# Attention and expert layer on one core: z products before block products, and 27 columns of counts moved behind the last numerators

## The chip, the cores and the metric

The kernel runs on one core of a Trainium2 chip. The metric is device time in microseconds of one execution, lower is better. Engines are named as the profile names them: PE (TensorE matmul), PEld (its weight load), DVE (VectorE), ACT (ScalarE), POOL (GpSimd), SP (SyncE, which here issues DMAs).

## The reference, cut to what matters

q, k and v have 8 batches, 8 heads, 576 positions and 64 channels; everything is float32.

```python
def phi(x):                                   # 64 -> 256 features
    proj = x @ w_phi                          # w_phi: 64 x 128
    proj = proj - max(abs(proj))              # over the 128 features
    return concat([exp(proj), exp(-proj)])
kv  = sum_s phi(k)[s,f] * v[s,d]              # block, 256 x 64, per head
z   = sum_s phi(k)[s,f]                       # 256, per head
out = (phi(q) @ kv) / (phi(q) @ z + 1e-6)     # numerator / denominator
x   = out as 4608 tokens x 512
# then an expert layer: logits = x @ w_gate (8 experts); tokens are given to experts in order of
# falling logit, 576 to each; out[token] = relu(x @ w1[e]) @ w2[e]
```

## The kernel before, in words

**Attention.** Two batches and two heads make one unit, 16 units in all (u = 0 to 15). A unit's steps carry short names, which the order table of the kernel uses too:

- `kt0`, `kt1`, `qt0`, `qt1`: DVE transposes of the loaded k and q (L178). `kg0`, `kg1`, `kg2` and `qg0`, `qg1`, `qg2`: PE projections, three groups of the nine positions tiles each (L189).
- `kgm`, `qgm`: DVE maximum (L194). `kgs2`, `qgs`: DVE subtraction (L197). For `kg0` and `kg1`, ACT copies out of PSUM (`kgc`, L203) and POOL subtracts (`kgs`, L206). `ke`: ACT exponentials (L218). `ad1` to `ad8`: POOL adds the nine tiles of phi(k) up (L226, L227), which is what z is made from.
- `kv0` to `kv2`: PE block sums over positions (L236). `kvt`: ACT copies them to SBUF as kvT (L240). `bd`: the block products, 32 PE instructions that spread the block and bring in the gate weights (L252). `kz`: ACT copies them into the tile kz (L255). `z`: the z products, 16 PE instructions of two columns (L265). `zk`: DVE puts z into the last column of kz (L267).
- `T0` to `T2`: PE transposes of q's projections (L281); `ex`: ACT exponentials (L285). `num0`, `num1`: the numerators with the denominator as their 73rd column (L298), which read kz. `x0`, `x1`: DVE division (L303 to L315); in the last unit ACT scales the rows instead (L314), reading the numerators from PSUM. `lg`: POOL adds the logits up. `st`: SP stores x.

Matmuls come in four shapes of the array: the page writes `64*64` (projections, kv, bd), `128*64` (z, numerators), `64*128` (T) and `128*8` (counts).

**Order.** All steps go into a planner (`Plan`, L18 to L99) with a due time from the table ATT; each engine executes its steps in the order of their due times, and a step whose inputs are late holds up everything behind it on its engine. In the steady stretch PE works on the projections of unit u+1 while it finishes unit u. PSUM is cut into four pairs of banks, g0 to g3; every PE step takes one pair, the one that by the plan comes free first (L93), and the pair is free again when its reader is done.

**The bridge to the experts.** The expert layer first sorts tokens by counting: digits of the logits are compared with thresholds, and PE counts the comparisons per expert. For the first 27 of the 36 columns of tokens (units 0 to 11) the comparisons are made by DVE while attention still runs (steps `pr0` to `pr5`, function prep0, L483 on). Their counts are the PE steps `cnt0`, `cnt1`, `cnt2` of nine matmuls each (L517), placed in attention's table, and the DVE step `n0` (L519) saves their sum. After the last numerators eleven matmuls of ones keep PE busy (`warm`, L321), while DVE makes x, logits and the comparisons of the last nine columns; then come nine counts (L517), whose result is compared with capacity less the saved sum (L639). Five further digits follow, each with 36 counts (L622), filler matmuls (`fill`, L588) and short DVE steps, until the first expert is known and its weights can be loaded. The eight experts' products (L935, L966, L981) fill the rest. The routing's PSUM tiles come from a pool that takes over attention's eight banks: the count tile (`rps`) lies in the banks that were g0, the filler's tile (`y1`) in a bank that was g1. A block of small DVE steps that prepares constants (`init`, L415 to L560) stands, by its due time, behind the last zk and ahead of the last x0.

Of the kernel before, what the change touches and what calls it, by code (L numbers as in the profile page):

```python
# [100 lines left out]
def attention(ctx, tc, nc, q, k, v, w_phi, w_gate, xs, L, C, xp, cfg={}, after=None, later=None, count=None, init=iter(())):  # L101
# [42 lines left out]
    def pair(u_):  # L144
        return lambda x: ps.tile([128,2,512],F32,name='g%d'%x['buf'][u_],bufs=1)
# [11 lines left out]
    def unit(u):  # L157
# [84 lines left out]
        add('kvt','ACT',ac(512),kend,kvt,[('kv',2)],frees=(('g',u,'kv'),))  # L242
        def bd(x):
            p=T['bdp',u]=pair(('g',u,'bd'))(x)
            t=T['kvT',u]
            for i in range(2):
                for fh in range(2):
                    for a in range(2):
                        r=slice(64*a,64*a+64)
                        for c in range(2):  # L250
                            o=128*fh+64*c
                            PE.matmul(p[64*c:64*c+64,a,72*(2*i+fh):72*(2*i+fh)+72],t[r,i,o:o+64],C['bd'][r,272*hp+72*i:272*hp+72*i+72],start=True,stop=True)  # L252
        def kz(x):
            t=T['kz',u]=sb.tile([128,2,2,2,73],F32,name='kz',bufs=2)
            A.copy(t.rearrange('p i h a e -> p a (i h) e')[:,:,:,0:72],T['bdp',u][:,:,0:288].rearrange('p a (g e) -> p a g e',e=72))  # L255
        add('bd','PE',520.,kend+d['bd'],bd,['kvt'],'Q',slots(('g',NG,'bd')),ins=65)
        add('kz','ACT',ac(576),kend+d['bd']+.6,kz,['bd'],slot=slots(('kz',2)),frees=(('g',u,'bd'),))
# [8 lines left out]
        def zk(x):  # L266
            V.tensor_copy(T['kz',u].rearrange('p i h a e -> p (h a) i e')[:,:,:,72],T['zp',u][:,0,0:8].rearrange('p (g i) -> p g i',i=2))  # L267
        add('z','PE',450.,kend+d['z'],z,[('ad',8)],'B',slots(('g',NG,'z')),(('ks',u),),ins=33)
        add('zk','DVE',180.,kend+d['z']+.5,zk,['z','kz'],frees=(('g',u,'z'),))
# [19 lines left out]
        for g,(j0,j1) in enumerate(JG):  # L289
            n=j1-j0; due=d['num']+d['ns']*g  # L290
            js=sorted(set(j//3 for j in range(j0,j1)))
            def pe(x,g=g,j0=j0,j1=j1):
                p=T['np',u,g]=pair(('g',u,'num',g))(x)
                for a in range(2):
                    for j in range(j0,j1):
                        for fh in range(2):
                            for ab in range(2):
                                PE.matmul(p[64*ab:64*ab+64,a,73*(j-j0):73*(j-j0)+73],T['qP',u,j//3][:,fh,a,ab,j%3,:],T['kz',u][:,a,fh,ab,:],start=fh==0,stop=fh==1)  # L298
            def dve(x,g=g,j0=j0,j1=j1,n=n):
                p=T['np',u,g][:,:,0:73*n].rearrange('p a (j e) -> p a j e',e=73)  # L300
                rd=sb.tile([128,2,n,1],F32,name='rd',bufs=2)
                if u==0 and g==0: sb.tile([128,8],F32,name='xpad',bufs=1)
                V.tensor_scalar(rd,p[:,:,:,72:73],1e-6,None,op0=OP.add)  # L303
                V.reciprocal(rd,rd)
                if g==0: T['x',u]=(xp if lastu else sb).tile([128,9,144],F32,name='xp',bufs=1 if lastu else 2)
                x_=T['x',u]
                Lb=L[:,9*bp+j0:9*bp+j1,:]
                if lastu:
                    L3=C['L3'][:,j0:j1]
                    for a in range(2): V.tensor_mul(L3[:,:,:,1+a],p[:,a,:,64*a:64*a+8],rd[:,a].to_broadcast([128,n,8]))  # L310
                    V.tensor_reduce(Lb.rearrange('p j (e o) -> p j e o',o=1),L3,axis=AX.X,op=OP.add)
                    if g==1: after()
# [22 lines left out]
        if u==NU-NP-1:  # L335

            it=later(); z0=t0+d['num']+d['ns']+d['pr']; prev=('lg',u)
            for i,(e,dur) in enumerate((('DVE',600.),('DVE',1500.),('POOL',100.),('DVE',350.),('DVE',1400.),('POOL',100.))):
                def f(x,it=it): next(it,None)
                P.add((('pr',i),u),e,dur,place(('pr',i),e,u,z0+d['prs']*i),f,[prev],lat=95. if e=='DVE' else 30.,lock=i in(1,4)); prev=(('pr',i),u)  # L340
            for c in range(NB-1):
                def cp(x,c=c):
                    if c==0: T['cnt']=ps.tile([128,2,512],F32,name='g%d'%x['buf'][('g',u,'cnt')],bufs=1)[0:8,0,0:32]
                    count[1](T['cnt'],c,count[4](c),c==0,c==NB-2)
                P.add((('cnt',c),u),'PE',600.,place(('cnt',c),'PE',u,z0+d['prs']*(6+c)),cp,[(('pr',4),u)]+([(('cnt',c-1),u)] if c else []),lat=200.,mode='Z',slot=(('g',NG,('g',u,'cnt')),) if c==0 else (),ins=18)
            P.add(('n0',u),'DVE',150.,place('n0','DVE',u,z0+d['prs']*(6+NB)),lambda x: count[2](T['cnt']),[(('cnt',NB-2),u)],lat=95.,frees=(('g',u,'cnt'),))
    for u in range(NU): unit(u)
    P.by[(('x',0),NU-1)]['deps'].append(('n0',NU-NP-1))
# [44 lines left out]
def moe_consts(rp, nc, C, L, MC, cfg={}):  # L393
# [31 lines left out]
    spacer=rp.tile([1,1],F32,name='spacer'); rp.tile([128,64],F32,name='mpad')  # L425
# [136 lines left out]
def moe(ctx, tc, nc, L, xs, w1, w2, out, C, MC, R0, rt, cfg={}):  # L562
# [11 lines left out]
    state,prep,(cmp0,cnt0,put0,prep0),DIG,KW,kt,kl,scl,k0,e8,ones,tri,dif,onef,msk,Q,dup,dup2,ids,half,un,opn,spacer,tin,eye8,e8s,pid=MC  # L574
# [14 lines left out]
    def routing(r):  # L589
# [3 lines left out]
        if not last:  # L593
# [415 lines left out]
def tile_kernel(ctx, tc, q, k, v, w_phi, moe_w_gate, moe_w1, moe_w2, out):  # L1009
# [59 lines left out]
```

## Time and profile before

| what | value |
|---|---|
| three timed runs | 752.07, 752.39, 754.91 us; median 752.39 us |
| the profiled execution | 754.1 us, of which the span of its instructions is 752.1 us |
| PE busy | 737.7 us (98%) |
| DVE busy | 564.4 us (75%) |
| ACT busy | 348.6 us (46%) |
| POOL busy | 307.0 us (41%) |
| mean granted PE clock | 0.994 of full speed |

Attention takes the first 268 us of the span, the routing's first expert about 30 us, the experts the rest. A busy share is an average over these stages; the last PE instruction of one step and the first of the next tell more, since PE executes in order: where start follows start without a gap, the difference of two starts is what a step costs.

### The profile page before, as it was taken

How to read it: one execution, taken by the hardware profiler on the slowest of the kernel's cores; microseconds unless marked ns; L12 is line 12 of the kernel's file. 1: busy time of each engine (PE TensorE's matmuls, PEld its weight loads, DVE VectorE, ACT ScalarE, POOL GpSimd, SP SyncE). 2: the span in 40 equal slices, each digit the busy share in tenths (PEclk: the TensorE clock that was granted, in tenths of full speed). 3: DMA queues.
4: the chain of work that ended last, by engine and by line, in shares of the span. 5: the costliest groups of instructions: out<-in, count | busy, mean ns of one | idle time of the engine just before them, and what ended most of it. 6: DMA issues, size and time to landing. Idle time of an engine off the chain costs nothing.

```text
span 752.1 us, 25412 instructions
## 1 busy us (share of the span) xinstructions
PE 737.7 (98%) x10898; PEld 634.0 (84%) x10899; DVE 564.4 (75%) x1487; ACT 348.6 (46%) x616; POOL 307.0 (41%) x329
## 2 busy tenths in 40 slices
PE   7999999999999999999999999999999999999997
PEld 4788898889888876888997997897897897897985
DVE  7989989998898868876895894895895895663410
ACT  3777777777776522513513513512522522532411
POOL 5998988988889503004104104104104104302002
PEclk9999999999999899999999999999999999999999
DMA  9988988888873114406305305406306407661301
GB/s 161 162 153 174 166 168 155 161 157 148 155 166 76 34 34 147 142 13 205 135 27 192 133 17 202 134 4 213 135 2 208 143 1 225 235 183 52 133 15 50
DMA packets 241168, 94.29 MB, mean 125 GB/s; under 512 B 190512, under 2 KB 227664, under 8 KB 241056
## 3 DMA queue, kind: packets, MB, share of 16 engines
q1 hardware_dynamic: 230288, 73.09, 40.9%
q0 software_dynamic: 6096, 18.98, 7.5%
q8 instruction: 86, 1.41, 0.8%
q10 hardware_dynamic: 4672, 0.59, 0.6%
q14 instruction: 26, 0.21, 0.1%
HBM read 72.58 MB, written 20.05 MB: 123 GB/s over the span
## 4 chain that ended last, share of the span: by engine, by line
PE 79%; issue 11%; DVE 4%; DMA 2%; ACT 2%; POOL 2%; POOLq 0%; SPq 0%; ACTq 0%; DVEq 0%
PE h L935 21%; PE y L966 18%; PE g L298 10%; PE g L236 8%; PE g L189 7%; PE g L281 3%; PE y L981 3%; PE g L252 2%; PE rps L627 2%; DMA raww<-in_moe_w_dram 1%; PE g L265 1%; PE h L900 1%; ACT kvT L240 1%; PE rps L622 1%; POOL out_dram L996 1%
## 5 line engine op out<-in xcount | busy, mean ns | idle before, releaser
L996 POOL DMA_INDIRECT out_dram<-ysb,idx x40 | 39.2, 979 | 330.7 <-ACT ysb L989 327.4
L227 POOL TENSOR_TENSOR ks<-ks,kP 128x512 f32<-128x512 f32 x112 | 143.4, 1281 | 7.1 <-ACT kP L218 0.8
L935 PE MATMUL h<-xh,w1l 128*128 128x272 f32 (+3 forms) x512 | 140.9, 295 | 1.2 <-DVE w1l L853 1.2
L935 PE MATMUL h<-xh,w1h 128*128 128x272 f32 (+3 forms) x512 | 141.0, 301 | 0.0
L948 ACT ACTIVATE fh<-h 128x240 fp32r<-128x240 f32 (+2 forms) x128 | 49.0, 385 | 131.1 <-PE h L935 118.1
L966 PE MATMUL y<-w2h,fh 128*128 128x512 f32 x256 | 100.8, 398 | 0.0
L966 PE MATMUL y<-w2h,fl 128*128 128x512 f32 x256 | 99.5, 393 | 0.0
L966 PE MATMUL y<-w2l,fh 128*128 128x512 f32 x256 | 99.5, 394 | 0.0
L935 PEld LDWEIGHTS h<-xh,w1l 128*128 128x128 f32 x512 | 96.3, 188 | 2.2 <-DVE w1l L853 1.4
L935 PEld LDWEIGHTS h<-xh,w1h 128*128 128x128 f32 x512 | 95.3, 188 | 2.2 <-issue 0.9
L935 PE MATMUL h<-xl,w1h 128*128 128x272 f32 (+3 forms) x512 | 93.2, 297 | 0.0
L218 ACT ACTIVATE kP<-kgt 128x768 f32<-128x768 f32 x96 | 74.1, 838 | 19.4 <-POOL kgt L206 19.4
L952 DVE SCALAR_TENSOR_TENSOR fl<-h,fh 128x240 fp32r<-128x240 f32 (+2 forms) x128 | 53.1, 417 | 37.4 <-ACT fh L948 19.5
L298 PE MATMUL g<-kz,qP 128*64 128x73 f32 x2304 | 79.8, 230 | 0.0
L298 PEld LDWEIGHTS g<-kz,qP 128*64 128x64 f32 x2304 | 77.1, 139 | 1.9 <-issue 0.9
L285 ACT ACTIVATE qP<-g 128x768 f32<-128x768 f32 x96 | 71.1, 815 | 13.6 <-PE g L281 13.4
L935 PEld LDWEIGHTS h<-xl,w1h 128*128 128x128 f32 x512 | 76.1, 188 | 0.5
L989 ACT COPY ysb<-y 128x512 f32<-128x512 f32 (+1 forms) x40 | 21.8, 546 | 110.8 <-issue 58.8
L236 PE MATMUL g<-kP,vi 64*64 64x256 f32 x1152 | 70.3, 377 | 0.0
L966 PEld LDWEIGHTS y<-w2h,fl 128*128 128x128 f32 x256 | 48.2, 188 | 9.2 <-issue 0.4
L966 PEld LDWEIGHTS y<-w2l,fh 128*128 128x128 f32 x256 | 48.2, 188 | 9.0
L966 PEld LDWEIGHTS y<-w2h,fh 128*128 128x128 f32 x256 | 48.2, 188 | 8.4
(224 smaller groups left out, 1313.8 us busy)
## 6 DMA issues: line engine op xcount, KB each, us to landing
raww<-in_moe_w_dram SPq DMA_DIRECT2D x64, 512.0 KB
vi<-in_v_dram SPq DMA_DIRECT2D x64, 144.0 KB
xs<-xp SPq DMA_DIRECT2D x32, 288.0 KB
ki<-in_k_dram SPq DMA_DIRECT2D x62, 144.0 KB
qi<-in_q_dram SPq DMA_DIRECT2D x62, 144.0 KB
xl<-xd SPq DMA_DIRECT2D x4, 288.0 KB
xd<-xg SPq DMA_DIRECT2D x4, 256.0 KB
xg<-xs,idx POOLq DMA_INDIRECT x40
```

What stands on the lines that cost most here:

```text
L189: PE.matmul(p[64*bi:64*bi+64,a,128*(s-s0):128*(s-s0)+128],t[r,bi,s,:],C['w'][r,:],start=True,stop=True)
L218: for i in range(2): A.activation(o[:,:,:,128*i:128*i+128],t,AF.Exp,scale=1.0-2*i)
L227: else: G.tensor_add(ks,ks,kP[:,s])
L236: PE.matmul(p[64*a:64*a+64,i,0:256],v_[r,a,s,:],kP[r,s,a,:],start=s==0,stop=s==8,skip_group_check=True)
L281: PE.transpose(p[:,i,o:o+64],t[r,a,s],ident[r,r])
L285: for fh in range(2): A.activation(t[:,fh].rearrange('p i a s t -> p i (a s t)'),p,AF.Exp,scale=1.0-2*fh)
L298: PE.matmul(p[64*ab:64*ab+64,a,73*(j-j0):73*(j-j0)+73],T['qP',u,j//3][:,fh,a,ab,j%3,:],T['kz',u][:,a,fh,ab,:],start=fh==0,stop=fh==1)
L935: PE.matmul(p,ws[:,k,o:o+128],xx[:,k,o1:o2],start=n==0,stop=n==11)
L948: A.activation(hh[:,f,o1:o1+m1],p[:,0:m1],AF.Relu)
L952: V.scalar_tensor_tensor(hl[:,f,o1:o1+m1],p[:,0:m1],0.0,hh[:,f,o1:o1+m1],op0=OP.max,op1=OP.subtract)
L966: PE.matmul(p,hx[:,f,o:o+128],ws[:,f%2,:],start=n==0,stop=n==23)
L996: st=G.indirect_dma_start(out=ov,out_offset=bass.IndirectOffsetOnAxis(ap=iv,axis=0),in_=yv,in_offset=None)
```

## The change

**In the units 3 to 13** (`zf`): z no longer stands behind bd, but ahead of it. bd waits for z, kz for zk, and zk no longer for kz; numerators wait for both. **At the end:** the steps cnt0, cnt1, cnt2, n0 and warm leave attention's table; behind the last numerators, the routing now issues the 27 counts, five filler matmuls of 512 columns (`idle(5)`) and then the last nine counts into one PSUM tile, and compares it with capacity directly. **The table ATT** has new due times throughout. MOE, the table of the experts, is the same.

```diff
-def attention(..., after=None, later=None, count=None, init=iter(())):
+def attention(..., after=None, later=None, init=iter(())):
...
+        zf=2<u<NU-2
+        def kzt():
+            if ('kz',u) not in T: T['kz',u]=sb.tile([128,2,2,2,73],F32,name='kz',bufs=2)
+            return T['kz',u]
...
-        add('bd','PE',520.,kend+d['bd'],bd,['kvt'],'Q',slots(('g',NG,'bd')),ins=65)
-        add('kz','ACT',ac(576),kend+d['bd']+.6,kz,['bd'],slot=slots(('kz',2)),frees=(('g',u,'bd'),))
+        add('bd','PE',520.,kend+d['bd'],bd,['kvt']+(['z'] if zf else []),'Q',slots(('g',NG,'bd')),ins=65)
+        add('kz','ACT',ac(576),kend+d['bd']+.6,kz,['bd']+(['zk'] if zf else []),slot=() if zf else slots(('kz',2)),frees=(('g',u,'bd'),))
...
-        add('zk','DVE',180.,kend+d['z']+.5,zk,['z','kz'],frees=(('g',u,'z'),))
+        add('zk','DVE',180.,kend+d['z']+.5,zk,['z'] if zf else ['z','kz'],slot=slots(('kz',2)) if zf else (),frees=(('g',u,'z'),))
...
-            add(('num',g),'PE',n*515.,due,pe,['zk']+[('ex',j) for j in js],'B',...)
+            add(('num',g),'PE',n*515.,due,pe,['zk','kz']+[('ex',j) for j in js],'B',...)
...
-        if lastu:
-            def wm(x):
-                p=pair(('g',u,'warm'))(x)
-                for _ in range(11): PE.matmul(p[:,0],w[:,0:128],w,start=True,stop=True)
-            P.add(('warm',u),'PE',2400.,1e6,wm,[(('num',1),u)],...)
...
-            for c in range(NB-1):
-                def cp(x,c=c): ...
-                P.add((('cnt',c),u),'PE',600.,place(('cnt',c),'PE',u,...),cp,...)
-            P.add(('n0',u),'DVE',150.,place('n0','DVE',u,...),lambda x: count[2](T['cnt']),...)
...
-    P.by[(('x',0),NU-1)]['deps'].append(('n0',NU-NP-1))
+    P.by[(('x',0),NU-1)]['deps'].append((('pr',5),NU-NP-1))
...
                 if part:
                     p=rps([8,K])
-                    cnt0(R,p,NT//9-1,cmp0(R,NT//9-1),True,True)
+                    for b in range(NT//9-1): cnt0(R,p,b,R['cm'][b],b==0,False)
+                    idle(5)
+                    cnt0(R,p,NT//9-1,cmp0(R,NT//9-1),False,True)
...
-                        if part: V.scalar_tensor_tensor(fl,p,-float(cap),R['n0'],op0=OP.add,op1=OP.is_ge,accum_out=da)
-                        else: V.tensor_scalar(fl,p,float(cap),0.0,op0=OP.is_ge,op1=OP.add,accum_out=da)
+                        V.tensor_scalar(fl,p,float(cap),0.0,op0=OP.is_ge,op1=OP.add,accum_out=da)
...
-ATT = {...}
+ATT = {...}
```

What the new due times of ATT mean, sorted for each engine (a name with ' is of the next unit):

```
one steady unit, PE
  before  kg0' qg0' kg2' kv0 kg1' kv1 qg2' kv2 qg1' bd z T2' T0' num0 num1 T1'
  after   kg0' kg2' kv0 kg1' qg2' kv1 qg0' kv2 qg1' z bd T2' T0' num0 num1 T1'
one steady unit, DVE (after)
          kgm0' kgm2' kgs2' kgm1' qgm2' qgs2' qgm0' qgs0' zk qgm1' kt0'' qgs1' kt1'' qt0'' x0 qt1'' x1
POOL      before  ad6 kgs0' ad7 ad8 kgs1' ad1'..ad5' lg
          after   ad6 lg(u-1) ad7 kgs0' ad8 kgs1' ad1'..ad5'
SP        before  ldk ldq ldv st;  after  ldk st ldq ldv; the k of unit 14 is loaded right behind
          that of unit 7 and transposed in units 6 and 10
the end, PE (unit number behind the @)
  before  num0@14 num1@14 T1@15 cnt0 bd@15 cnt1 cnt2 z@15 T2@15 num0@15 num1@15 warm
  after   bd@14 bd@15 T0@14 z@14 T1@15 qg2@15 T2@14 num0@14 num1@14 T0@15 T2@15 z@15 num0@15 num1@15
the end, DVE (after)
          zk@14 qgm2@15 pr3 pr4 qgs2@15 x0@14 x1@14 zk@15 init x0@15 x1@15
```

## Rows read from the trace of the kernel before

**Rows 1.** Busy time by stretch: start:end, length, engines' busy us, clock, DMA.
```profile
20.00:40.00 20.00, 18.37 (x536) 15.97 (x532) 19.83 (x30) 15.04 (x21) 18.49 (x15) 1.00 0.91 163
97.74:113.20 15.46, 15.41 (x448) 13.73 (x445) 13.96 (x21) 11.65 (x16) 13.41 (x11) 1.00 0.86 168
```

**Rows 2.** Timeline of one steady unit: start us, busy us, engine, line, instructions.
```profile
67.51 0.83 PE L189 MATMUL g<-w,qT 64*64 64x128 f32 x24
...
68.17 0.83 PE L189 MATMUL g<-w,kT 64*64 64x128 f32 x24
...
71.13 2.64 POOL L227 TENSOR_TENSOR ks<-ks,kP 128x512 f32<-128x512 f32 x2
...
74.02 0.83 PE L189 MATMUL g<-w,qT 64*64 64x128 f32 x24
...
74.90 0.58 PEld L252 LDWEIGHTS g<-bd,kvT 64*64 64x64 f32 x32 [0.29 <-ACT kvT L240]
...
75.56 0.63 PE L265 MATMUL g<-sel,ks 128*64 128x2 f32 x16
75.70 0.65 ACT L255 COPY kz<-g 128x576 f32<-128x576 f32 x1 [0.85 <-PE g L252]
...
76.13 0.96 PE L281 MATMUL g<-ident,qgt 64*128 64x64 f32 x24
...
77.02 4.80 PE L298 MATMUL g<-kz,qP 128*64 128x73 f32 x144
...
81.75 0.58 PE L281 MATMUL g<-ident,qgt 64*128 64x64 f32 x12
```

**Rows 3.** Waits of the weight loads, 82 to 236 us: total, times, longest.
```profile
PEld g L252 <- ACT kvT L240: 2.9, 10, 0.3
```

**Rows 4.** PE timeline of unit 0: block products followed by the same shape.
```profile
21.02 0.73 PE L252 MATMUL g<-bd,kvT 64*64 64x72 f32 x32 [0.70 <-ACT kvT L240]
21.57 1.49 PE L189 MATMUL g<-w,kT 64*64 64x128 f32 x48
```

**Rows 5.** PE timeline from the end of unit 14's numerators to the last counts.
```profile
255.75 0.59 PE L281 MATMUL g<-ident,qgt 64*128 64x64 f32 x12
256.26 0.70 PE L517 MATMUL g<-cmp,OH 128*8 128x32 bf16 x9
257.18 0.73 PE L252 MATMUL g<-bd,kvT 64*64 64x72 f32 x32 [0.21 <-DVE rd L303]
257.84 1.26 PE L517 MATMUL g<-cmp,OH 128*8 128x32 bf16 x18
259.03 1.02 PE L265 MATMUL g<-sel,ks 128*64 128x2 f32 x16
259.98 0.90 PE L281 MATMUL g<-ident,qgt 64*128 64x64 f32 x12
260.81 7.21 PE L298 MATMUL g<-kz,qP 128*64 128x73 f32 x144
267.95 2.55 PE L321 MATMUL g<-warm 128*128 128x512 bf16 x10
270.73 0.71 PE L517 MATMUL rps<-cmp,OH 128*8 128x32 bf16 x9 [0.23 <-DVE cmp L514]
```

**Rows 6.** Busy time by stretch, as in rows 1, of the last unit.
```profile
259.00:266.00 7.00, 7.00 (x116) 6.84 (x116) 3.89 (x30) 1.51 (x2) 0.00 (x0) 0.51 0.38 87
```

**Rows 7.** Timeline of DVE and ACT in the last unit.
```profile
260.17 0.22 DVE L415 TENSOR_SCALAR kl<-ktf 128x128 bf16<-128x128 f32 x1
...
263.73 0.20 DVE L560 CAST ids<-idp 128x72 bf16<-128x72 int32 x1
...
266.87 3.79 ACT L314 ACTIVATE xp<-g,rd 128x64 f32<-128x64 f32 x18 [4.37 <-DVE L L310]
...
268.06 0.17 DVE L303 TENSOR_SCALAR rd<-g 128x8 f32<-128x8 f32 x1 [0.91 <-PE g L298]
...
269.12 0.23 DVE L438 TENSOR_REDUCE m<-L 128x9 f32<-128x72 f32 x1
```

More of the change, by code (lines that the diff above doesn't have):

```diff
@@ L99, in order, with attention @@
         return sorted(out,key=lambda x:(x['start'],x['n']))
-def attention(ctx, tc, nc, q, k, v, w_phi, w_gate, xs, L, C, xp, cfg={}, after=None, later=None, count=None, init=iter(())):
+def attention(ctx, tc, nc, q, k, v, w_phi, w_gate, xs, L, C, xp, cfg={}, after=None, later=None, init=iter(())):
     B,H,S,D=q.shape
@@ L253, in kz @@
         def kz(x):
-            t=T['kz',u]=sb.tile([128,2,2,2,73],F32,name='kz',bufs=2)
+            t=kzt()
             A.copy(t.rearrange('p i h a e -> p a (i h) e')[:,:,:,0:72],T['bdp',u][:,:,0:288].rearrange('p a (g e) -> p a g e',e=72))
-        add('bd','PE',520.,kend+d['bd'],bd,['kvt'],'Q',slots(('g',NG,'bd')),ins=65)
-        add('kz','ACT',ac(576),kend+d['bd']+.6,kz,['bd'],slot=slots(('kz',2)),frees=(('g',u,'bd'),))
+        add('bd','PE',520.,kend+d['bd'],bd,['kvt']+(['z'] if zf else []),'Q',slots(('g',NG,'bd')),ins=65)
+        add('kz','ACT',ac(576),kend+d['bd']+.6,kz,['bd']+(['zk'] if zf else []),slot=() if zf else slots(('kz',2)),frees=(('g',u,'bd'),))
         def z(x):
@@ L266, in zk @@
         def zk(x):
-            V.tensor_copy(T['kz',u].rearrange('p i h a e -> p (h a) i e')[:,:,:,72],T['zp',u][:,0,0:8].rearrange('p (g i) -> p g i',i=2))
+            V.tensor_copy(kzt().rearrange('p i h a e -> p (h a) i e')[:,:,:,72],T['zp',u][:,0,0:8].rearrange('p (g i) -> p g i',i=2))
         add('z','PE',450.,kend+d['z'],z,[('ad',8)],'B',slots(('g',NG,'z')),(('ks',u),),ins=33)
-        add('zk','DVE',180.,kend+d['z']+.5,zk,['z','kz'],frees=(('g',u,'z'),))
+        add('zk','DVE',180.,kend+d['z']+.5,zk,['z'] if zf else ['z','kz'],slot=slots(('kz',2)) if zf else (),frees=(('g',u,'z'),))
         blocks('q',d['qaft'])
@@ L315, in dve @@
                 else: V.tensor_mul(x_[:,j0:j1].rearrange('p j (a e) -> p a j e',a=2),p[:,:,:,0:72],rd.to_broadcast([128,2,n,72]))
-            add(('num',g),'PE',n*515.,due,pe,['zk']+[('ex',j) for j in js],'B',slots(('g',NG,'num',g)),tuple(('qP',u,j) for j in js)+(('kz',u),),ins=32*n)
+            add(('num',g),'PE',n*515.,due,pe,['zk','kz']+[('ex',j) for j in js],'B',slots(('g',NG,'num',g)),tuple(('qP',u,j) for j in js)+(('kz',u),),ins=32*n)
             add(('x',g),'DVE',(430+dv(144*n)) if not lastu else 900.,due+2.7,dve,[('num',g)],seq=('x',0) if g else None,slot=slots(('xb',2)) if g==0 else (),frees=(('g',u,'num',g),))
-        if lastu:
-            def wm(x):
-                p=pair(('g',u,'warm'))(x)
-                for _ in range(11): PE.matmul(p[:,0],w[:,0:128],w,start=True,stop=True)
-            P.add(('warm',u),'PE',2400.,1e6,wm,[(('num',1),u)],lat=0.,mode='W',slot=(('g',NG,('g',u,'warm')),),frees=(('g',u,'warm'),),ins=11)
         def st(x):
@@ L340, in unit @@
                 P.add((('pr',i),u),e,dur,place(('pr',i),e,u,z0+d['prs']*i),f,[prev],lat=95. if e=='DVE' else 30.,lock=i in(1,4)); prev=(('pr',i),u)
-            for c in range(NB-1):
[L342 to L346, printed above, removed]
     for u in range(NU): unit(u)
-    P.by[(('x',0),NU-1)]['deps'].append(('n0',NU-NP-1))
+    P.by[(('x',0),NU-1)]['deps'].append((('pr',5),NU-NP-1))
     NI=18
@@ L424, in moe_consts @@
     onef=C['one']
-    spacer=rp.tile([1,1],F32,name='spacer'); rp.tile([128,64],F32,name='mpad')
+    spacer=rp.tile([1,1],F32,name='spacer'); rp.tile([128,96],F32,name='mpad')
     half=rp.tile([128,1],F32,name='half'); un=rp.tile([128,NT],F32,name='un'); opn=rp.tile([128,8],F32,name='opn')
@@ L517, in cnt0 @@
         for j in range(9): nc.tensor.matmul(p,R['OH'][:,9*bp+j,:],cmp[:,:,j],start=first and j==0,stop=last and j==8)
-    def put0(R,p):
-        R['n0']=rp.tile([8,KW[0]],F32,name='n0'); V.tensor_scalar(R['n0'],p,-1.0,None,op0=OP.mult)
     def state():
         return dict(m=S([128,NT,1],'m'),dg=S([128,ND,NT],'dg',BF),sm=S([128,NT,1],'sm',BF),OH=S([128,NT,8],'OH',BF))
-    MC.extend((state,prep,(cmp0,cnt0,put0,prep0),DIG,KW,kt,kl,scl,k0,e8,ones,tri,dif,onef,msk,Q,dup,dup2,ids,half,un,opn,spacer,tin,eye8,e8s,pid))
+    MC.extend((state,prep,(cmp0,cnt0,prep0),DIG,KW,kt,kl,scl,k0,e8,ones,tri,dif,onef,msk,Q,dup,dup2,ids,half,un,opn,spacer,tin,eye8,e8s,pid))
     yield
@@ L573, in mid @@
     def mid(x,t): return x[:,None,:].to_broadcast([x.shape[0],t,x.shape[1]])
-    state,prep,(cmp0,cnt0,put0,prep0),DIG,KW,kt,kl,scl,k0,e8,ones,tri,dif,onef,msk,Q,dup,dup2,ids,half,un,opn,spacer,tin,eye8,e8s,pid=MC
+    state,prep,(cmp0,cnt0,prep0),DIG,KW,kt,kl,scl,k0,e8,ones,tri,dif,onef,msk,Q,dup,dup2,ids,half,un,opn,spacer,tin,eye8,e8s,pid=MC
     ND=len(DIG)
@@ L1026, in init @@
         for _ in moe_consts(rp, nc, C, L, MC, {'lat0': 2.95, 'latr': 2.33, 'latc': 1.56, 'slack': 0.66, 'slack1': -0.2, 'pre': 0, 'warm': 44, 'wide': 1, 'latd': 0.46, 'lq': 0.96, 'lo': 0.49, 'lm': 1.69, 'lat7': 3.76, 'lgh': 1.56, 'lgx': 1.29, 'xs': 13, 'xb': 3, 'c0': 1, 'x0': 7, 'w0v': 1, 'xn': 4, 'w2o': 22, 'hc': 272, 'r1d': 1.56, 'w2s': 10, 'r1s': 0.0}):
-            if MC and not R0: R0.update(MC[0]())
+            if MC and not R0: R0.update(MC[0](), n0=True)
             yield
     def prep():
-        yield from MC[2][3](R0, 27)
+        yield from MC[2][2](R0, 27)
     def after():
@@ L1039, in tile_kernel @@
     with ExitStack() as actx:
-        attention(actx, tc, nc, q, k, v, w_phi, moe_w_gate, xs, L, C, xp, ATT, after, prep, tuple(lambda *x, i=i: MC[2][i](R0, *x) for i in range(4)) + (lambda c: R0['cm'][c],), init())
+        attention(actx, tc, nc, q, k, v, w_phi, moe_w_gate, xs, L, C, xp, ATT, after, prep, init())
     moe(ctx, tc, nc, L, xs, moe_w1, moe_w2, out, C, MC, R0, rt, {'lat0': 2.95, 'latr': 2.33, 'latc': 1.56, 'slack': 0.66, 'slack1': -0.2, 'pre': 0, 'warm': 44, 'wide': 1, 'latd': 0.46, 'lq': 0.96, 'lo': 0.49, 'lm': 1.69, 'lat7': 3.76, 'lgh': 1.56, 'lgx': 1.29, 'xs': 13, 'xb': 3, 'c0': 1, 'x0': 7, 'w0v': 1, 'xn': 4, 'w2o': 22, 'hc': 272, 'r1d': 1.56, 'w2s': 10, 'r1s': 0.0})
```

2 lines of the change are left out of this document (1 added, 1 removed).

## The prediction

> **What bounds the kernel now.** I began with the busy time by stretches. A steady unit takes 15.46 us and PE is busy for 15.41 of them; DVE follows with 13.96 [rows 1]. So in the steady stretch the period is PE's own work, and a saving counts only if it shortens PE's line. The timeline of one unit shows what that line holds. The reader should subtract starts: a set of 24 projections takes 0.66 us (67.51 to 68.17), but the set ahead of the block products takes 0.88 (74.02 to 74.90), and the weight load of bd says why: it waits for ACT's kvT [rows 2]. PE's busy time hides this, because the modelled end of the last projection covers it. The view of waits confirms ten such waits in the steady stretch, 2.9 us together, up to 0.3 each [rows 3].
>
> Then the end of attention, read as a timeline. From the end of unit 14's numerators (255.75) to that of unit 15's (267.95) PE needs 12.20 us. Two pieces are counts: 0.92 us from 256.26 to 257.18 and 1.19 from 257.84 to 259.03 [rows 5]. Behind them everything is slow: z takes 0.95 (259.03 to 259.98), the transposes 0.83 and the numerators 7.14, where the same steps take 0.57 and 4.73 in the steady unit, and 0.51 for a group of twelve transposes at 255.75 [rows 2, 5]. The stretch view gives the reason: from 259 to 266 the granted clock is 0.51, the lower of its two levels (1.2 of 2.4 GHz), right after the counts [rows 6]. After the numerators DVE alone sets the pace: from its first step on the second numerators (268.06) to the next counts (270.73) pass 2.67 us [rows 5, 7].
>
> **Steady units.** From qg1' to the transposes PE now spends 74.02 to 76.13, 2.11 us. Afterwards the order is qg1', z, bd. qg1' costs 0.66. bd among matmuls of its own shape takes 0.55 (21.02 to 21.57), and 0.66 where z's shape follows, so leaving a shape costs 0.11 [rows 2, 4]. The new line is 0.66 + 0.11 (to z) + 0.57 (z, which pays its own leaving) + 0.55 + 0.11 (bd, to the transposes) = 2.00. bd's input is ready 0.88 after qg1' starts, and bd now starts 1.34 after it, so the wait is covered with 0.46 to spare. The gain is 0.11 if each switch costs 0.11, and 0.22, the whole wait, if the added one is free. I take 0.15, nearer to the dear end because that is a row. Ten units (3 to 12) give 1.5 us, bounds 1.1 and 2.2.
>
> The change adds one change of shape to each unit. The Trainium skill says, on the page TensorEngine Tiling (Array Packing), section Key Properties, that changing the tiling mode drains the engine, which speaks against the new order; it gives no time for it. Rows 2 and 4 agree that a switch costs, with 0.11 us; if the drain cost as much as the wait, 0.22, the sum would be 749.8 instead of 748.3.
>
> What hides the rest: kz starts 0.80 after bd and lasts 0.65, done at 1.45; numerators come 0.66 + 0.89 = 1.55 behind bd's start, so kz is covered by 0.10. Without cover it costs what it is late by. zk moves from behind kz to behind z and is early. On DVE, zk stands ahead of qgm1', the transposes and x0; DVE can wait 15.46 - 13.96 - 0.15 = 1.35 us a unit there before it sets the period. z needs ad8: before, the two last adds end at 73.77 (71.13 + 2.64), and z's new place is 74.79; POOL's new order puts one add, not two, behind kgs0'. For SP, store and loads change places and one of two k buffers is held from unit 7 to 10; the DMA engines are 0.86 busy, 13.3 of 15.46 us [rows 1], so some 2 us of standing still a unit are free. Other orders inside the projections are of one shape and cost nothing while DVE frees the banks.
>
> **Start.** The first units run at DVE's pace: 19.83 of 20 us from 20 to 40, with PE busy 18.37 [rows 1]. The new table changes the order there and no work. I take 0, between -1.6 (all of PE's idle time in that stretch) and +1.6 (as much again).
>
> **End of attention.** Removed: 0.92 + 1.19 = 2.11 us of counts. With the counts gone nothing light stands between the numerators, so I expect the higher clock: z 0.95 - 0.57, transposes 0.83 - 0.51, numerators 7.14 - 4.73, together 3.11. Added: T0@15 now follows the numerators of unit 14 and num0@15 needs its exponential, a pair of 1.51 us on ACT (the only ACT work in rows 6); T2 (0.51) and z (0.57) cover 1.08, so PE waits about 0.5 with the hand-over. DVE has init between zk and x0@15, 3.76 us (260.17 to 263.93), and each x step is 1.06 (268.06 to 269.12) [rows 7]; from z's start this is about 0.8 + 3.76 + 1.06 = 5.6, against PE's 0.57 + 0.5 + 4.73 = 5.8, but pr4, qgs2@15 and the x steps of unit 14 are queued ahead of zk, so I put DVE 0.4 late (0 to 0.8). Sum: 2.11 + 3.11 - 0.5 - 0.4 = 4.3 us earlier.
>
> The 27 counts cost 1.19/18 = 0.066 each, 1.8 us, and five fillers 2.55/11 = 0.23 each, 1.15 us (the code issues eleven) [rows 5]. Together 2.95 us behind the last numerators (call their end N). DVE has its compare ready at N + 0.5 + 2.67 = N + 3.2, so the counts lie under DVE's chain with 0.2 to spare. n0 and the different comparison cost the same on DVE. The experts' table is the same and moves as a whole.
>
> **Sum.** 754.1 (profiled execution) - 1.5 - 0 - 4.3 = 748.3 us. The median of the runs, 752.39, is 1.7 below the profiled one; part of it may be that the low clock is shorter in other runs, part the profile itself. The changed kernel has no low stretch in this forecast, so I keep 748.3 and let the low end take 752.39 - 5.8 - 0.7 (the cheap switches) = 746.0 in.
>
> **Rivals.** *The counts meet ACT in the banks.* The routing's count tile lies in the banks of one pair, its filler tile in another, and num0@15 and num1@15 hold two of the four until ACT has read them: 18 instructions in 3.79 us, 0.21 each [rows 7]. x0 now ends right ahead of x1, so I estimate the reading from N + 0.5 to N + 4.3, the first ten (num0's) to N + 2.6. If the count tile lies with num1, the last counts come at 4.3 + 2.95 = N + 7.25 instead of 3.2, 4.0 later; with num0, 2.3 later; the filler tile alone with num1 2.2, with num0 0.5. Of twelve ways to lie, four cost 0.5 or nothing, five 2.2 or 2.3, three 4.0. Before, the nine counts began 0.07 after ACT's last reading (270.66) and 0.05 after their compare, so the rows allow both. Time 750.6, at worst 752.3.
>
> *The low clock moves into the routing*, since 27 small matmuls now stand just ahead of it. For it: it fell right behind the same counts [rows 6]. Against it: the counts follow full numerators and fillers follow them. If it cost what it costs now, 3.1, the time is 751.4. The Trainium skill, TensorE: Matmul & The Clock Gate, section What's actually happening, says the default is the throttled state and activity releases it; rows 6 agree with a fall to 0.51 behind light work, and by that rule alone the sum would be this 751.4.
>
> *z ahead of bd brings nothing:* switches and a late kz eat the 0.22; 749.8.
>
> *Slower: DVE stands still in front of zk.* zk now heads DVE's queue before z is done, with qgm1', four transposes and x0 behind it, and those free PE's banks and feed its next unit. Up to 1.35 us a unit this is free; beyond it every microsecond costs 10 over ten units. From 2.3 us on (0.96 over) the gain of 5.8 and 3.8 more are lost: 757.9. For it: DVE's 90%. Against it: ad8 was done 1.0 us ahead of z's new place.
>
> **Chances.** Forecast 0.42; banks 0.35; clock 0.08; z brings nothing 0.08; slower 0.07. About 0.5% (3.8 us) can be told from no change: faster is below 748.6, slower above 756.2. The forecast lies close to that edge; I count 0.36 of it as faster, and 0.08 from the others, where the profiled time overstates the runs. Faster 0.44, same 0.48, slower 0.08. The range runs from 746.0 to the worst bank case, 752.3.
>
> **What would show it.** Units of 15.3 us, and no wait of bd for kvT; clock 1.00 from 240 to 270; last numerators about 6 us earlier (near 262), and the counts of the last nine columns about 3.2 behind their end. A wait of the first counts on ACT would show the bank rival; a clock of 0.5 in the routing the second; numerators waiting for kz the third; DVE waiting for L265 by more than 1.35 us a unit the last. A start of the steady stretch later than now by over 1.6 us would make the sum wrong at its least worked term.

## The result, and the profile after

The changed kernel is slower: median 760.49 us of seven runs (758.79 to 764.00), beside 752.39 us for seven runs of the kernel before; ratio 1.0119, 95% interval 1.0099 to 1.0139. The forecast was 748.3 us, the range 746.0 to 752.3. The profiled execution took 759.36 us, its span is 757.1 us. The ratios leave out one execution, 1184.35 us at a granted clock of 0.556, of the last experiment below. In this profile z is L269, bd L256, T L285, the numerators L302, ACT's scaling L318, the counts L510, the five fillers `idle` L575.

First the steady stretch. Two windows of the changed kernel, columns as in [rows 1], then PE's timeline:

```profile
104.69:121.42 16.73, 16.05 (x449) 14.55 (x445) 14.82 (x23) 11.56 (x17) 13.68 (x13) 1.00 0.92 176
152.28:167.62 15.34, 15.34 (x448) 13.73 (x444) 14.27 (x22) 11.44 (x17) 13.68 (x12) 1.00 0.83 158
```

```profile
103.92 0.83 PE L189 MATMUL g<-w,qT 64*64 64x128 f32 x24
104.69 0.63 PE L269 MATMUL g<-sel,ks 128*64 128x2 f32 x16
105.25 0.73 PE L256 MATMUL g<-bd,kvT 64*64 64x72 f32 x32
105.91 0.96 PE L285 MATMUL g<-ident,qgt 64*128 64x64 f32 x24
```

From qg1' to the transposes PE now spends 103.92 to 105.91, 1.99 us (forecast 2.00; before 2.11 [rows 2]), and an undisturbed unit takes 15.34 us, not 15.46 [rows 1]. So the exchange works. But one unit takes 16.73. SP and DVE, in the same execution:

```profile
93.03 7.81 SPq L125 DMA_DIRECT2D ki<-in_k_dram  x8
100.93 2.14 SPq L325 DMA_DIRECT2D xs<-xp  x2
103.11 5.58 SPq L125 DMA_DIRECT2D qi<-in_q_dram  x4
```

```profile
110.86 0.78 DVE L178 STREAM_TRANSPOSE qT<-qi 128x576 f32<-128x576 f32 x1 [1.60 <-DMA qi<-in_q_dram]
```

SP issues the k of units 7 and 14 in one go (eight transfers), then a store, and q of unit 7 only at 103.11; DVE waits 1.60 us for it, and PE behind DVE.

Then the end of attention, PE:

```profile
231.25 4.80 PE L302 MATMUL g<-kz,qP 128*64 128x73 f32 x144
238.06 0.89 PE L189 MATMUL g<-w,qT 64*64 64x128 f32 x24 [2.01 <-ACT kgt L203]
239.45 1.29 PE L189 MATMUL g<-w,kT 64*64 64x128 f32 x24 [0.51 <-DVE xp L319]
240.44 4.17 PE L236 MATMUL g<-kP,vi 64*64 64x256 f32 x48
...
256.96 4.80 PE L302 MATMUL g<-kz,qP 128*64 128x73 f32 x144
...
263.59 4.98 PE L302 MATMUL g<-kz,qP 128*64 128x73 f32 x144 [0.37 <-DVE kz L271]
271.88 1.80 PE L510 MATMUL rps<-cmp,OH 128*8 128x32 bf16 x27 [3.32 <-ACT xp L318]
273.62 2.06 PE L575 MATMUL y<-onesb 128*128 128x512 bf16 x5
275.61 0.71 PE L510 MATMUL rps<-cmp,OH 128*8 128x32 bf16 x9
```

The reader should see two places. Behind the numerators of unit 13, PE stands 2.0 and 0.5 us, and the kv products that follow take 4.17 us for 48, at a granted clock of 0.60 (2.77 us in the run with POOL's pr2 moved, below). Behind the last numerators the 27 counts wait 3.32 us for ACT's line L318; the last nine come at 275.61, where before they came at 270.73 [rows 5]. The windows and ACT's row:

```profile
240.00:244.00 4.00, 4.00 (x57) 3.26 (x53) 3.89 (x7) 3.05 (x4) 3.35 (x5) 0.60 0.31 67
...
272.00:278.00 6.00, 6.00 (x52) 3.69 (x51) 1.33 (x9) 0.00 (x0) 0.00 (x0) 0.72 0.42 98
```

```profile
268.04 3.79 ACT L318 ACTIVATE xp<-g,rd 128x64 f32<-128x64 f32 x18 [2.80 <-DVE L L314]
```

What stood ahead of PE's 2.0 us is on DVE, beside POOL:

```profile
231.55 1.26 DVE L488 TENSOR_TENSOR di<-s,s 128x27 int32<-128x27 int32 x1
233.22 1.80 DVE L492 TENSOR_SCALAR di<-s 128x27 int32<-128x27 int32 x5
235.05 1.26 DVE L493 TENSOR_TENSOR dg<-di,scl 128x135 bf16<-128x135 int32 x1
...
272.62 0.33 DVE L507 TENSOR_TENSOR cmp<-dg,k 128x288 bf16<-128x288 bf16 x1 [1.65 <-PE rps L510]
```

```profile
231.48 1.30 POOL L227 TENSOR_TENSOR ks<-ks,kP 128x512 f32<-128x512 f32 x1
233.44 1.47 POOL L206 TENSOR_TENSOR kgt<-kgt,kgm 128x768 f32<-128x768 f32 x1 [0.66 <-ACT kgt L203]
234.87 1.29 POOL L227 TENSOR_TENSOR ks<-ks,kP 128x512 f32<-128x512 f32 x1
```

These are steps of pr1 (L485 to L493), which the new table puts 16 us earlier (before, pr1 began at 247.15). The two of 1.26 us, and the one of the five L492 that took 1.48, each end with an instruction of POOL, within 0.15 us (231.55 + 1.26 = 232.81, POOL 231.48 + 1.30 = 232.78). pr1 takes 5.3 us (230.89 to 236.2). Behind it on DVE stands the maximum of kg1 of unit 15 (L194), and behind that ACT's copy (L203), for which PE waits the 2.0 us.

### The profile page after: what moved, and what is told of

It reads as the page before. It is cut to its first block, busy times and chain, and to the rows that moved or that the text cites. A ratio compares the mean times of both kernels' runs of the same rounds, so it can differ in the third digit from the quotient of the medians.

```text
span 757.1 us, 25418 instructions
## 1 busy us (share of the span) xinstructions
PE 736.6 (97%) x10893; PEld 637.2 (84%) x10893; DVE 569.7 (75%) x1486; ACT 346.3 (46%) x616; POOL 305.5 (40%) x329
## 4 chain that ended last, share of the span: by engine, by line
PE 76%; issue 12%; DVE 4%; SPq 3%; DMA 2%; POOL 2%; ACT 1%; POOLq 0%; DVEq 0%; ACTq 0%
PE h L927 21%; PE y L958 18%; PE g L302 8%; PE g L236 7%; PE g L189 7%; PE y L973 3%; PE g L285 3%; SPq L125 2%; PE rps L620 2%; DMA raww<-in_moe_w_dram 1%; SPq L132 1%; PE g L256 1%; PE g L269 1%; PE h L892 1%; PE rps L615 1%
## 5 line engine op out<-in xcount | busy, mean ns | idle before, releaser
L302 PE MATMUL g<-kz,qP 128*64 128x73 f32 x2304 | 78.1, 227 | 0.8 <-DVE kz L271 0.4
L218 ACT ACTIVATE kP<-kgt 128x768 f32<-128x768 f32 x96 | 75.7, 848 | 5.6 <-POOL kgt L206 3.4
L302 PEld LDWEIGHTS g<-kz,qP 128*64 128x64 f32 x2304 | 75.0, 136 | 2.9 <-issue 0.9
L236 PE MATMUL g<-kP,vi 64*64 64x256 f32 x1152 | 72.8, 383 | 0.7 <-PE g L189 0.4
L236 PEld LDWEIGHTS g<-kP,vi 64*64 64x64 f32 x1152 | 47.2, 135 | 12.1 <-DMA vi<-in_v_dram 0.8
```

Of the source, the lines that this page charges most:

```text
L218: for i in range(2): A.activation(o[:,:,:,128*i:128*i+128],t,AF.Exp,scale=1.0-2*i)
L236: PE.matmul(p[64*a:64*a+64,i,0:256],v_[r,a,s,:],kP[r,s,a,:],start=s==0,stop=s==8,skip_group_check=True)
```

## The experiments

Ratios are to the kernel before, timed on the same chip, in brackets their 95% interval. Where two runs are compared by their ratios, the difference is uncertain by about 0.002 to 0.003, 1.5 to 2 us.

**z and bd alone.** On the kernel before, its own table:

```diff
-        return u*16.+t[...]
+        if 2<u<NU-3 and name in('bd','z'): name='z' if name=='bd' else 'bd'
+        return u*16.+t[...]
...
-add('zk',...,['z','kz'],...)   add('kz',...,['bd'],...)   add('bd',...,['kvt'],...)
+add('zk',...,['z'],...)        add('kz',...,['bd','zk'],...)   add('bd',...,['kvt','z'],...)
```

> The kernel before, with its own table; in units 3 to 12 z and bd only exchange places. Theory A (the exchange is worth what the steady units of the changed kernel show, 15.34 us against 15.465): ten units give 1.25 us, up to 1.5, so 751.0 us where the kernel before shows 752.4, and steady units of 15.34 us. Theory B (the exchange costs something elsewhere, and part of the changed kernel's loss is its): not faster than the kernel before, units of 15.46 us or more.

Measured: 751.32 us, 0.9993 [0.9981, 1.0004]; units of 15.46 us: theory B. DVE and PE of one unit (here z is L270, zk L272, T L286):

```profile
107.19 0.94 DVE L195 TENSOR_REDUCE qgm<-g 128x6 f32<-128x768 f32 x1
108.06 0.16 DVE L272 COPY kz<-g 128x8 f32<-128x8 f32 x1
```

```profile
107.78 1.08 PE L286 MATMUL g<-ident,qgt 64*128 64x64 f32 x24
108.78 4.80 PE L303 MATMUL g<-kz,qP 128*64 128x73 f32 x144
```

The two groups of transposes take 1.00 us (107.78 to 108.78) instead of 0.89. By the kernel's plan the second group has the pair of banks of z, and zk empties it only at 108.22 (108.06 + 0.16), because qgm1' stands ahead of it. So zk was moved too:

```diff
-        return u*16.+t[...]
+        return u*16.+t[...]-(1.8 if name=='zk' and 2<u<NU-3 else 0.)
```

> As in the run that only exchanged z and bd in units 3 to 12, on the kernel before and its table; here DVE's step zk also moves ahead of the next unit's qgm1, as the changed kernel has it. Theory A (there the second transposes waited for the pair of banks that z holds until zk has read it, and zk stood behind qgm1): the wait of 0.11 goes, units of 15.34 to 15.36 us, 1.1 to 1.25 us faster than before, 750.6. Theory B (z ahead of bd is worth nothing; the shorter units of the changed kernel come from its other orders): units of 15.46 us, 751.8.

Measured: 751.49 us, 0.9989 [0.9976, 1.0002]. Undisturbed units take 15.34 (185.54 to 200.88, for one): theory A for the unit. Of the 1.25 us only some 0.8 show in the ratio, and the interval holds 1.0, so that no gain of the whole kernel is shown; in this profile four other units were 0.2 to 1.5 us longer, with waits for which the trace names no releaser. Why is open.

**The counts alone**, as the changed kernel has them, in the table and z order of the kernel before:

```diff
-        zf=2<u<NU-2
+        zf=False
-ATT = {...}   # of the changed kernel
+ATT = {...}   # of the kernel before
```

> The kernel before, with its own table and its own order of z and bd; only the 27 counts, the five fillers and the last nine counts stand where the changed kernel has them. Theory A (the new place of the counts loses behind the last numerators nearly what it gives ahead of them): the last numerators end 5.2 us earlier (2.1 of counts and 3.1 of low clock), and the last counts come 7.3 us behind them, not 2.8, so 0.7 us faster than before, 751.7. Theory B (the loss at the end belongs to the new table alone): the last counts come at about 3.2 us behind the numerators, 4 us faster than before, 748.4.

Measured: 753.92 us, 1.0025 [1.0012, 1.0039]: 1.9 us slower, where both theories had it faster. The mechanism is that of theory A:

```profile
268.18 1.80 PE L510 MATMUL rps<-cmp,OH 128*8 128x32 bf16 x27 [3.03 <-ACT xp L318]
269.92 2.31 PE L575 MATMUL y<-onesb 128*128 128x512 bf16 x5
272.17 0.71 PE L510 MATMUL rps<-cmp,OH 128*8 128x32 bf16 x9
```

Last counts 7.1 us behind the numerators' end (265.1). What failed in the expectation is the gain set against it, 3.1 us of low clock; see below.

**Are these the banks?** The changed kernel, its pairs of banks laid elsewhere by the order in which they are first used:

```diff
-    p=ps.tile([128,2,512],F32,name='g0',bufs=1)
+        p=ps.tile([128,2,512],F32,name='g%d'%(0,3,2,1)[min(i,3)],bufs=1)
```

> The changed kernel with attention's pairs of banks laid elsewhere: the last numerators lie in banks 4 to 7, the routing's count tile in bank 0 and its filler tile in bank 2, so that none of them shares a bank with what ACT reads last. Theory A (the wait is made bank by bank, as the prediction's bank rival has it): the first count does not wait for ACT, the last counts come 3.3 us earlier, 757.2. Theory B (the new pool's first tile waits for the last reader of the old pool as a whole, whichever bank it reads): the first count still waits about 3.3 us for ACT's line L318 or its counterpart, 760.5.

Measured: 764.14 us, 1.0143 [1.0119, 1.0168], and the wait stays:

```profile
281.97 1.81 PE L511 MATMUL rps<-cmp,OH 128*8 128x32 bf16 x27 [3.32 <-ACT xp L319]
```

Theory B. In both layouts the first tile of the new pool waits 3.32 us, to the end of the old pool's last reader. It shows even without this run: by its own plan the changed kernel has its last numerators in the pairs g2 and g1, and the count tile lies in what was g0, so there too the first count shared no bank with what ACT read last. (This execution is long for other causes: it starts 6 us later, and its long unit takes 20.0 us.)

**The counts in attention's own banks**, in the changed kernel:

```diff
-    P.add((('cnt',c),u),'PE',600.,place(('cnt',c),'PE',u,...),cp,[(('pr',4),u)]+...
+    P.add((('cnt',c),u),'PE',600.,1e6+c,cp,[(('pr',4),u),(('num',1),NU-1)]+...
-    P.add(('n0',u),'DVE',150.,place('n0','DVE',u,...),...
+    P.add(('n0',u),'DVE',150.,1e6,...
-    for _ in range(11): PE.matmul(p[:,0],w[:,0:128],w,start=True,stop=True)   # warm
+    for _ in range(5): PE.matmul(p[:,0],w[:,0:128],w,start=True,stop=True)
```

> The changed kernel with its table and its order of z and bd; the 27 counts and the five fillers stand behind the last numerators as there, but in a pair of attention's own banks, and their sum is saved by the step n0 as in the kernel before; only the last nine counts use the routing's tile. Theory A (the first count's wait for ACT is what makes the end late): the 27 counts start right behind the numerators, the last nine wait only for ACT's last reading, 3.5 us behind the numerators instead of 7.3; 3.7 us faster than the changed kernel, 756.8. Theory B (the end is late because DVE or a low clock is): the last counts stay about 7 us behind the numerators, 760.5.

Measured: 756.79 us, 1.0064 [1.0044, 1.0083]: theory A. The counts start right behind the numerators, the last nine 3.4 us behind, at a clock of 1.00 from 263 to 276:

```profile
268.29 1.81 PE L521 MATMUL g<-cmp,OH 128*8 128x32 bf16 x27
...
271.68 0.71 PE L521 MATMUL rps<-cmp,OH 128*8 128x32 bf16 x9 [0.40 <-ACT xp L318]
```

**pr1 and POOL.** Two ways of keeping them apart. First POOL's pr2, which waits for pr1, ahead of ad1 of unit 14:

```diff
+ATT['o']['s']['pr2.POOL'] = 122.3   # was 258.2
```

> The changed kernel with one step moved: POOL's pr2, which waits for pr1, stands ahead of ad1 of unit 14, so that POOL stands still while DVE does pr1 in its early place. Theory A (single steps of pr1 wait for the POOL add that runs beside them): the five operations L492 take 0.5 us instead of 1.8, the two tensor operations 0.2 and 0.3 instead of 1.26 each, pr1 about 2.1 us instead of 5.3; PE's wait of 2.0 us at 236 shrinks by what POOL's later adds don't take back, 0 to 2 us faster than the changed kernel. Theory B (these operations are long by themselves at this place): they keep 1.26 and 1.8 us.

Measured: 757.45 us, 1.0063 [1.0044, 1.0081], more than expected. DVE and POOL:

```profile
233.92 0.19 DVE L488 TENSOR_TENSOR di<-s,s 128x27 int32<-128x27 int32 x1
...
234.50 0.50 DVE L492 TENSOR_SCALAR di<-s 128x27 int32<-128x27 int32 x5
235.04 0.30 DVE L493 TENSOR_TENSOR dg<-di,scl 128x135 bf16<-128x135 int32 x1
```

```profile
235.41 0.18 POOL L495 COPY hold<-dg 1x1 bf16<-1x1 bf16 x1 [3.77 <-DVE dg L493]
```

Theory A: same place, no POOL instruction beside it, 0.19, 0.50 and 0.30 us. PE's waits at 236 and 239 are gone with it, and so is the low clock: from unit 13's numerators to unit 14's it is 21.35 us (234.00 to 255.35), not 25.71 (231.25 to 256.96). Second, pr1 late:

```diff
+ATT['o']['s'].update({'pr0.DVE': 124., 'pr1.DVE': 144., 'pr2.POOL': 204.})
```

> The changed kernel with the comparisons' first two steps later on DVE (pr0 behind qgs1 of unit 15, pr1 behind kgs2 of unit 15, 12 us later) and POOL's step pr2 ahead of ad3 of unit 15, so that POOL stands still while pr1 runs, as in the kernel before. Theory A (pr1 early, among POOL's adds, takes 5.3 us of DVE instead of 2.05, makes PE wait 2.0 and 0.5 us at 236 to 240, and the low clock behind it costs 1.9): pr1 takes about 2.1 us, the wait and the low clock from 240 to 243 go, the last numerators end 3 to 4 us earlier, 757. Theory B (PE's wait there comes from ACT's copies or from bank order, not from pr1): same time as the changed kernel, 760.5.

Measured: 759.29 us, 1.0091 [1.0066, 1.0115]. The early waits go (239.41 follows the numerators without a gap), but PE meets DVE later, and unit 14's numerators take 5.48 us, at a granted clock of 0.84 from 258 to 264; 23.83 us between the two numerators. Half a cure at best: the interval overlaps the changed kernel's.

**The loads.** Three due times of unit 14's k put back to those of other units:

```diff
+ATT['o']['8'].update({'ldk.SP': 46.56, 'kt0.DVE': 18.41, 'kt1.DVE': 19.07})
```

> The changed kernel with three due times of unit 14 put back to those of the steady units: the load of its k on SP and the two transposes of it on DVE. Theory A (the one long steady unit, 16.73 us, is made by k of unit 14 ahead of q of unit 8 in SP's queue): that unit takes 15.34 like the others, 1.4 us faster than the changed kernel, 759.1; up to 2.1 us if the short wait for v near 223 us goes too. Theory B (the unit is long for another cause, such as DVE's queue): the same time as the changed kernel, 760.5.

Measured: 762.20 us, 1.0144 [1.0119, 1.0169]. Theory A is right of the unit (15.36, 105.30 to 120.66; the q that waits in the changed kernel is that of unit 7, not 8) and wrong of the sum, which is no gain: unit 14's k is back in its late place, and PE now waits 3.80 us for a load of v there:

```profile
224.75 4.02 PE L236 MATMUL g<-kP,vi 64*64 64x256 f32 x23 [3.80 <-DMA vi<-in_v_dram]
```

Then the same early load put into the kernel before:

```diff
+ATT['o']['8'].update({'ldk.SP': -104.3, 'kt0.DVE': -93.0, 'kt1.DVE': -30.4})
```

> The kernel before with one thing of the changed kernel's table: k of unit 14 is loaded right behind k of unit 7, ahead of q of unit 7, and transposed there (first half ahead of unit 7's transposes, second half behind zk of unit 9). Theory A (the load's place in SP's queue and the k buffer that it holds until unit 10 are what makes one steady unit of the changed kernel 1.4 to 5 us long): one or two units near 95 to 125 us are longer by that, 1.4 to 5 us slower than before, 753.4 to 757. Theory B (the DMA engines have 2 us of slack a unit and hide it): 752.0, no change.

Measured: 751.88 us, 0.9998 [0.9983, 1.0013]. Theory B: the early load alone costs nothing that these runs show (the interval is 1.1 us to either side). The kernel before issues q of unit 7 at 91.38 and uses it at 109.55, 18.2 us later:

```profile
91.38 4.10 SPq L125 DMA_DIRECT2D qi<-in_q_dram  x4
```

```profile
109.55 0.74 DVE L178 STREAM_TRANSPOSE qT<-qi 128x576 f32<-128x576 f32 x1
```

With k of unit 14 ahead of it, 13.3 us are left (98.97 to 112.30), and DVE doesn't wait. In the new table with the late k (the run before this one) q is issued at 99.47 and used at 109.14, 9.7 us later; with the early k, in the changed kernel, it is issued at 103.11 and DVE stands. The load of another unit costs only where q has little lead. This run also shows what I had not known of the kernel before, its counts and all behind them at full clock:

```profile
261.11 1.26 PE L517 MATMUL g<-cmp,OH 128*8 128x32 bf16 x18
262.30 0.63 PE L265 MATMUL g<-sel,ks 128*64 128x2 f32 x16
262.87 0.59 PE L281 MATMUL g<-ident,qgt 64*128 64x64 f32 x12
263.38 4.80 PE L298 MATMUL g<-kz,qP 128*64 128x73 f32 x144
...
271.49 0.70 PE L517 MATMUL rps<-cmp,OH 128*8 128x32 bf16 x9 [0.82 <-ACT xp L314]
```

**The cures together.** Own banks and pr2, in the changed kernel:

> The changed kernel with two edits of earlier runs together: the 27 counts in attention's own banks (which alone gave a ratio of 1.0064 to the kernel before), and POOL's pr2 ahead of ad1 of unit 14 (which alone gave 1.0063; the changed kernel has 1.0119). Theory A (the two losses are separate, one behind the last numerators and one ahead of them): the gains of 4.1 and 4.2 us add up, ratio 1.0008, about 752.6 us. Theory B (both cure the same microseconds): ratio 1.006, about 756.5.

Measured: 751.64 us, 0.9995 [0.9978, 1.0011]: theory A. Then the loads as well, q ahead of the store and unit 14's k behind both:

```diff
+ATT['o']['s']['ldq.SP'] = 53.5
+ATT['o']['8'].update({'ldk.SP': -56.0, 'kt0.DVE': -77.7})
```

> The changed kernel with the two cures that together gave 0.9995, and a third: in SP's queue q of a unit stands ahead of the store of an earlier unit, k of unit 14 comes behind q of unit 7 and that store instead of ahead of them, and DVE transposes its first half ahead of unit 8's k. Theory A (the long unit is DVE's wait for q of unit 7, which the new table issues 9.7 us ahead of its use, where the kernel before does it 18.2 us ahead, so that 4 us of another load in between are too many): the unit that took 20.4 us in the run with two cures takes 15.34, up to 5.0 us less in the profile, 1.4 to 5 us in the runs, 746.6 to 750.2. Theory B (k of unit 14 takes a k buffer and DMA time wherever it stands, and the stall moves to another load): 751.6, no change.

Measured: 748.02 us, 0.9955 [0.9941, 0.9969]: theory A, and faster than both kernels. SP now has q of unit 7 ahead of unit 14's k, and that unit takes 15.34 us (104.28 to 119.62):

```profile
93.88 4.48 SPq L125 DMA_DIRECT2D qi<-in_q_dram  x4
98.46 1.31 SPq L330 DMA_DIRECT2D xs<-xp  x2
99.81 4.58 SPq L125 DMA_DIRECT2D ki<-in_k_dram  x4
```

**The two ideas in the old table.** Kernel before, z ahead of bd and zk ahead of qgm1' as in the second experiment, counts in attention's own banks:

> The kernel before with its own table and the change's two ideas: z ahead of bd in units 3 to 12 with zk ahead of qgm1 (which alone gave 0.9989), and the 27 counts behind the last numerators in attention's own banks, then five fillers. Theory A (the counts ahead of z and T cost PE 2.1 us there; behind the numerators they lie under DVE's chain, and what comes back is 0.66 of waits for exponentials and zk and 0.3 of ACT ending later): 0.5 + 1.1 = 1.6 us faster than before, 750.3. Theory B (the last counts wait for ACT as before, and the low clock comes behind the counts wherever they stand): 0.5 us faster or less, 751.5.

Measured: 749.80 us, 0.9966 [0.9953, 0.9979]; theory A, a little better than worked out. From unit 14's numerators to the last counts it is 15.67 us (251.43 to 267.10); with the counts at their old place it is 17.21 (254.28 to 271.49 in the run with the early load).

```profile
263.95 1.81 PE L522 MATMUL g<-cmp,OH 128*8 128x32 bf16 x27
265.69 1.25 PE L326 MATMUL g<-warm 128*128 128x512 bf16 x5
267.10 0.70 PE L522 MATMUL rps<-cmp,OH 128*8 128x32 bf16 x9
```

## Why the prediction was wrong

**Steady units: right.** 15.34 against a forecast of 15.31; PE's line from qg1' to the transposes is 0.12 us shorter, as if the added switch of shape cost the 0.11 us of [rows 2, 4], so half of the 0.22 us of waiting is kept. The drain that the Trainium skill names (TensorEngine Tiling (Array Packing), Key Properties) did not cost the whole wait, by which the sum would have been 749.8. The rival that z ahead of bd brings nothing needed one more condition, which the first run showed: it is true as long as zk stays behind qgm1'.

**"For SP ... some 2 us of standing still a unit are free": failed.** The slack of the DMA engines (0.86 busy) is not the slack of one load. What counts is the time from a load's issue to its use, 18.2 us before and 9.7 in the new table; with eight transfers and a store in between, q came late. The term was put at nothing. It cost 1.4 us in the profile, 5.0 in the profile of the run with two cures (104.87 to 125.25; of the six profiled executions with this order two show 1.4 to 1.6 us and four 4.4 to 5.0), and 0.0040 of the time, 3.0 us, between the runs with two and with three cures. The lead can be read from the new due times; I costed the queue's order and not the lead.

**Start: right** (0.9 us earlier, bounds 1.6).

**End of attention, "0.4 late" on DVE: failed as the whole price of DVE's new order.** I named pr4 as queued ahead of zk and put what moving pr0 and pr1 does at nothing. Behind zk the 0.4 was enough: PE waits 0.37 us for zk, and ACT's reading begins at 268.04, no later than the numerators end. The loss lies 30 us earlier. At its new place pr1 runs beside POOL's adds and subtraction and takes 5.3 us instead of 2.05, the copy of kg1 for unit 15 stands behind it, PE stands 2.5 us, and a low clock behind it costs 1.7 (from 239.45 to 244.40 it is 4.95 us, where the run with pr2 ahead takes 3.25, 239.44 to 242.69, for the same work). Taking it away gave 1.0119 - 1.0063, 4.2 us. On the Trainium skill's page SBUF — State Buffer, section Who interferes with whom, DVE and POOL share a port pair under an exclusive lock, and a tensor_tensor with both inputs in SBUF contends with POOL's reads. The trace agrees: the tensor_tensor L488 took 1.26 us beside a POOL add and 0.19 without. One tensor_scalar of L492, with one input, took 1.48 us instead of 0.17 as well, which that sentence on tensor_tensor does not cover.

**The counts: the rival's price was right, its rule and its chance were not.** "4.0 later" for the count tile in the wrong banks; in the profile it is 3.7 (from the start of the last numerators to the last nine counts 12.02 us, 263.59 to 275.61, and 8.30 with own banks, 263.38 to 271.68), in the runs 1.0119 - 1.0064, 4.1 us. Without the wait the last counts come 3.4 us behind the numerators, where the forecast had 3.2. But I took it for a lottery of twelve ways to lie, four of them harmless. In both layouts the count tile lay apart from the last numerators and still waited: the pool's hand-over waited for the last reader as a whole. The rows before allowed that: the first routing count stands 0.07 us behind ACT's last reading, and in the run with the early load it waits 0.82 us for ACT. And which pairs the numerators have could have been read from the plan. A second wait stands behind the first: the fourth comparison has the buffer of the first (three buffers), so DVE waits 1.65 us for the counts. It costs nothing more here, because the last nine counts stand behind the fillers.

**"Numerators 7.14 - 4.73 ... together 3.11": a term that most runs don't have.** It was read from one execution whose mean granted clock is 0.994. Seven microseconds at 0.51 lower the mean of 752 us by 0.0046 (worked out from [rows 6]). Of the 78 runs of the kernel before that were timed beside the experiments none is below 0.996, and 52 are at 0.998 or above, which leaves no room for such a stretch. With the same counts at the same place the clock is 1.00 in the run with the early load. So the counts alone don't make the low clock in [rows 6], and taking them away wins no 3.1 us in most runs; moving them to the right place wins 17.21 - 15.67 = 1.5. I saw that the profiled execution stood 1.7 above the median and put the excess into the low end of the range; it belonged out of the sum.

**The low clock that moves into the routing** came in part, behind something else: in the changed kernel PE stands 3.3 us first, and the five fillers then take 2.06 us instead of 1.25 and the next six 1.34 instead of 0.83. With the counts right behind the numerators the clock stays at 1.00. The page of the Trainium skill that I cited for this rival, TensorE: Matmul & The Clock Gate, section What's actually happening, says that activity releases the throttle. Here the fall came behind idle time, and light matmuls alone left the clock at 1.00 in the run with the early load; what made the fall of [rows 6] stays open.

In one sum, from the median run of before: -1.25 for ten units, +1.4 to +5.0 for the long one, +4.2 for pr1, and for the counts -1.5 + 4.1 = +2.6 (alone, in the old table, +1.9), together +7.0 to +10.6, or +6.1 to +9.7 with the 0.9 us of the start; measured +8.1 (medians), 8.9 by the ratio. The range is that of the long unit. With the three costs taken away the same idea takes 748.0 us. That is close to the 748.3 of the forecast, but in part by luck: the forecast subtracted 3.1 us of low clock from a profiled execution that stood 1.7 above the median, and the faster start is not in it.

What stays open: the units that are 0.2 to 1.5 us longer without a cause in the trace, why the long unit costs 1.4 us in one execution and 5 in another, and why the clock fell behind pr1's wait in one execution and not in another.

## What to carry to other kernels

When a whole table of due times is new, look at it step by step: for each load the time from issue to use, and for each moved step on DVE what POOL does beside it. Here the first tile of a new pool waited for the last reader of the old one, wherever it lay, so work that is to run right behind a stage belongs in that stage's own buffers. Take a term out of a sum if it comes from the state of the one profiled execution: compare its clock with the clocks of the timed runs first.

## What the runs showed of the hardware

DVE operations of 0.17 to 0.30 us became 1.26 and 1.48 us beside POOL instructions of 1.29 to 1.47, and each ended within 0.15 us of POOL's. The granted clock fell to 0.60 behind 2.0 us of PE idle in one run (240 to 244 us) and stayed at 1.00 behind the same idle in another (the run with the counts in own banks, 236 to 244 us).
